# Two units' scores together in six PSUM banks: the order of scores and values in a top-k attention kernel with an MLP

## The chip, the cores and the metric

The kernel runs on one core of a Trainium2 chip. A core has a matrix engine (PE) that writes its results into PSUM, a vector engine (DVE), an activation engine (ACT), a general engine (POOL) and DMA queues, here all issued by the sync engine (SP). Each engine works through its own list of instructions in order and waits on semaphores for the others. PSUM has eight banks of 512 float32 per partition; a tile pool of the kernel hands them out in whole banks.

The metric is the device time of one execution in microseconds. The kernel before takes 1516.82 us (median of four runs, 1515.82 to 1518.07). The profile comes from one further look at the same program: that execution took 1517.07 us, of which 1515.2 us are the span that the profile shows.

## What is computed

Eight batches of eight heads, 576 queries and keys of 64 elements each. Of each row of scores the 32 largest are kept, the rest are masked; softmax, times the values; the heads side by side make a token of 512, and the 4608 tokens go through a leaky-ReLU MLP of width 2048. Everything is float32.

```python
scores = scale * np.matmul(q, k.transpose(0, 1, 3, 2))          # (8, 8, 576, 576)
kth = np.partition(scores, -32, axis=-1)[..., -32:-31]
scores = np.where(scores >= kth, scores, -1e9)
attn = np.exp(scores - np.max(scores, axis=-1, keepdims=True))
attn = attn / (np.sum(attn, axis=-1, keepdims=True) + 1e-09)
x = np.matmul(attn, v)                                          # to (4608, 512)
h = x @ w_in                                                    # 512 to 2048
out = np.maximum(0.01 * h, h) @ w_out                           # 2048 to 512
```

## The kernel before, in words

**Units.** The attention is cut into 144 units. A unit is a pair of heads and 128 queries (or 64 queries of two pairs, for the 64 queries that are left over in each batch). The steps of the main loop (`for s in range(...)`, L416) each work on several units at once: in step s, DVE selects the top 32 of unit s (`top_k`), POOL masks unit s-1 (`mask`), ACT takes exponents of unit s-1 (`exponents`, `sums`), normalises unit s-2 (`normalize`, after DVE's `reciprocals`) and splits it into 16-bit halves (`transpose`), which SP writes to DRAM and reads back transposed as `wT`. On every even step PE multiplies two transposed units with their values (`weigh_values`), ACT copies the result into the MLP's input (`keep_values`), and PE computes the scores of two later units, s+2 and s+3 (`scores`).

**Scores.** The two heads of a unit lie on rows 0 to 63 and 64 to 127 of the matrix engine and run side by side. Head i writes the tile `psc{i}`, two banks with 288 keys each, and ACT copies each head with one instruction of 576 columns into the unit's SBUF tile `s_sb`. There is one pair of these tiles (four banks), so the second unit's scores can't start before the first unit's copies are done. The kernel puts the values between the two: first unit's scores, values of two units, second unit's scores (L449 to L459).

**MLP.** `mlp` (L299) is a generator that issues a few matmuls at a time. For a chunk of 256 tokens (the first two have 128) it forms 16 hidden blocks: four matmuls into a bank `ph` (L307), then one ACT instruction `Prelu` into `gT` (L313). Then for each 128 tokens 16 matmuls of 512 columns into a bank `pz` (L319), an ACT copy to `o_sb` (L326) and a DMA out. A float32 matmul of the program stands in the trace as two MATMUL records. `mlp_steps` spreads these pieces over seven slots of each step, by a budget; five of the slots come before the scores and values of an even step, two after. PE therefore leaves a hidden block half done at a slot's end, does the scores and values, and takes it up again.

**Banks.** Four for the scores, one for the values (`ps_po`, tile `po`), three in turn for the MLP (`ps_ml`, tag `ml`). The MLP's next tile waits until ACT has emptied the tile three before it.

**Order.** The whole order is written by hand (`tc.manual_schedule`): each engine gets its instructions in the order of the program text. On ACT an even step reads: two normalisations (L250), the exponents of head 0 (L238), two splits (L259), the exponents of head 1 with the sums (L238, L243), then copies of scores and values, with the `Prelu` of each finished hidden block standing where its last matmuls were issued. So ACT can't empty a bank while it is still at an earlier normalisation or split.

**Before the loop** the MLP's weights, 16 pieces given as float64, are rounded to float32 (`round_weights`). The first 13 pieces use the score banks, the last three the MLP's. The scores of units 0 and 1 are issued at piece 14 of 0 to 15 (L409).

## Time and profile before

| What | Value |
|---|---|
| median of four runs | 1516.82 us |
| the profiled execution | 1517.07 us |
| its span | 1515.2 us |
| DVE busy | 1330.7 us (88%) |
| ACT busy | 1118.1 us (74%) |
| POOL busy | 1079.4 us (71%) |
| `ph` matmuls, L307 | 2432 records, 517.1 us |
| `pz` matmuls, L319 | 1152 records, 506.7 us |
| scores, L198 | 1280 records, 199.4 us; idle before them 28.3 us |
| values, L283 | 3200 records, 182.6 us; idle before them 20.4 us |
| `Prelu` of 256 columns, L313 | 272 of 380 ns |
| copy of 512 columns out of PSUM, L326 | 36 of 586 ns |
| copy of one head's scores, L207 | 288 of 639 ns |

Matmul records overlap: the engine takes the next one before the last has left its pipeline. The time that a matmul costs is therefore read from start to start, and a PE that shows as 100% busy may still hide gaps of a tenth of a microsecond.

### The profile page before, as it was taken

What the parts mean: (1) busy time and instruction counts of PE and PEld (TensorE: products, weight loads), DVE (VectorE), ACT (ScalarE), POOL (GpSimd) and SP (SyncE); (2) the same over time, 40 slices, a digit from 0 to 9 for tenths busy, and PEclk for the clock granted to TensorE, in tenths of its full rate; (3) what the DMA queues carried; (4) which work ended last, traced back from release to release, by engine and by line L of the source; (5) the groups of instructions that cost most, each with busy time, mean ns of one, the idle gap of its engine ahead of it and who ended that gap; (6) DMA issues with size and microseconds to landing.
All of it is one profiled execution on the core that took longest, in us unless ns stands there. A gap on an engine that the chain in (4) does not pass through costs nothing.

```text
span 1515.2 us, 24441 instructions
## 1 busy us (share of the span) xinstructions
PE 1431.4 (94%) x8192; PEld 952.6 (63%) x8192; DVE 1330.7 (88%) x3421; ACT 1118.1 (74%) x2141; POOL 1079.4 (71%) x726
## 2 busy tenths in 40 slices
PE   6736978999999999999999999999999999999998
PEld 2324665757676766575757676767676666666774
DVE  6799999999899998899999998999999989999600
ACT  7846787878787877687878787878787878787720
POOL 0068778887878777878787777777887878788700
PEclk9965989999999999999999999999999999999999
DMA  7714456555765455545655455645665456544510
GB/s 285 280 31 125 126 153 185 165 140 141 186 152 150 128 166 157 167 133 151 176 165 135 140 160 168 166 136 148 192 153 149 139 155 154 154 135 138 140 54 14
DMA packets 399294, 227.05 MB, mean 150 GB/s; under 512 B 343360, under 2 KB 343360, under 8 KB 397120
## 3 DMA queue, kind: packets, MB, share of 16 engines
q1 hardware_dynamic: 399168, 225.49, 53.3%
q8 instruction: 64, 1.05, 0.3%
q14 instruction: 62, 0.51, 0.1%
HBM read 46.14 MB, written 94.37 MB: 93 GB/s over the span
## 4 chain that ended last, share of the span: by engine, by line
PE 82%; DVE 11%; ACT 4%; DMA 2%; issue 1%; SPq 0%; POOL 0%; DVEq 0%; ACTq 0%; POOLq 0%
PE ph L307 31%; PE pz L319 30%; PE psc L198 10%; PE po L283 10%; DVE tops L221 4%; DVE pairs L224 3%; DVE pairs L216 1%; ACT split L259 1%; DMA raw<-in_weights_dram 1%; ACT s_sb L238 1%; ACT s_sb L250 1%; DVE scale L144 1%; ACT wT L121 0%; DVE w_out L147 0%; ACT scale L127 0%
## 5 line engine op out<-in xcount | busy, mean ns | idle before, releaser
L234 POOL TENSOR_SCALAR pen<-s_sb,tops 128x576 f32<-128x576 f32 x288 | 638.4, 2217 | 237.6 <-DVE tops L221 204.4
L221 DVE MAX8 tops<-pairs 128x8 f32<-128x288 f32 (+1 forms) x1152 | 635.5, 591 | 0.0
L307 PE MATMUL ph<-x,w_in 128*128 128x256 f32 (+1 forms) x2432 | 517.1, 372 | 6.4 <-ACT gT L313 6.4
L319 PE MATMUL pz<-w_out,gT 128*128 128x512 f32 x1152 | 506.7, 595 | 1.3 <-ACT gT L313 1.3
L307 PEld LDWEIGHTS ph<-x,w_in 128*128 128x128 f32 x2432 | 442.3, 192 | 87.0 <-issue 21.9
L224 DVE MATCH_REPLACE8 pairs<-tops,pairs 128x288 f32<-128x288 f32 (+1 forms) x864 | 459.8, 537 | 0.0
L235 POOL TENSOR_TENSOR s_sb<-s_sb,pen 128x576 f32<-128x576 f32 x288 | 406.8, 1413 | 24.0
L319 PEld LDWEIGHTS pz<-w_out,gT 128*128 128x128 f32 x1152 | 215.9, 190 | 265.4 <-issue 263.0
L259 ACT COPY split<-s_sb 128x1152 uint16<-128x1152 uint16 x288 | 315.6, 1144 | 0.0
L207 ACT COPY s_sb<-psc 128x576 f32<-128x576 f32 x288 | 169.3, 639 | 114.7 <-PE psc L198 114.7
L250 ACT ACTIVATE s_sb<-s_sb,rz 128x576 f32<-128x576 f32 x288 | 206.6, 767 | 31.8 <-DVE rz L247 31.7
L238 ACT ACTIVATE s_sb<-s_sb,nbias 128x576 f32<-128x576 f32 x288 | 221.1, 768 | 11.5 <-POOL s_sb L235 11.4
L198 PE MATMUL psc<-kt,qt 64*128 64x288 f32 (+1 forms) x1280 | 199.4, 442 | 28.3 <-ACT s_sb L207 27.8
L216 DVE TENSOR_TENSOR pairs<-s_sb 128x576 f32<-128x576 f32 x288 | 213.7, 780 | 10.2 <-DVE tops L221 0.5
L283 PE MATMUL po<-wT,vt 128*64 128x128 f32 (+1 forms) x3200 | 182.6, 271 | 20.4 <-DMA wT<-apart 19.6
L283 PEld LDWEIGHTS po<-wT,vt 128*64 128x64 f32 x3200 | 163.7, 141 | 52.2 <-issue 27.6
L313 ACT ACTIVATE gT<-ph 128x256 f32<-128x256 f32 (+1 forms) x304 | 107.3, 369 | 100.9 <-PE ph L307 100.6
L198 PEld LDWEIGHTS psc<-kt,qt 64*128 64x128 f32 (+1 forms) x1280 | 110.9, 182 | 100.4 <-ACT s_sb L207 37.2
L232 POOL TENSOR_SCALAR nbias<-tops 128x2 f32<-128x2 f32 x144 | 33.5, 233 | 92.3 <-DVE tops L221 79.5
L247 DVE RECIPROCAL rz<-ze 128x2 f32<-128x2 f32 x144 | 22.4, 155 | 74.4 <-ACT ze L243 73.8
L297 ACT COPY x<-po 128x128 f32<-128x128 f32 (+1 forms) x160 | 32.5, 264 | 65.6 <-PE po L283 65.6
L224 DVE MATCH_VALUE_LOAD pairs<-tops,pairs 128x8 f32 x864 | 62.0, 72 | 0.0
(38 smaller groups left out, 317.2 us busy)
## 6 DMA issues: line engine op xcount, KB each, us to landing
apart<-split SPq DMA_DIRECT2D x288, 288.0 KB, 2.1
raw<-in_weights_dram SPq DMA_DIRECT2D x16, 1024.0 KB, 5.0
vt<-in_vk_dram SPq DMA_DIRECT2D x32, 320.0 KB, 3.7
qt<-in_qT_dram SPq DMA_DIRECT2D x32, 288.0 KB, 3.6
kt<-in_kT_dram SPq DMA_DIRECT2D x32, 288.0 KB, 4.0
out_dram<-o_sb SPq DMA_DIRECT2D x36, 256.0 KB, 2.0
wT<-apart SPq DMA_TRANSPOSE x144, 4.6
```

Source lines behind the costliest of these rows:

```text
L198: nc.tensor.matmul(ps[i][r0:r0 + u.rows, half, 0:HS], qt[d, u.q0:u.q0 + u.rows], kt[d, half * HS:(half + 1) * HS], start=True, stop=True,)
L216: nc.vector.tensor_tensor(pairs[:, :, n, :], u.both[:, :, 0:HS], u.both[:, :, HS:S], op)
L221: nc.vector.max(out=u.tops[:, i, r, :], in_=rest[i])
L224: nc.vector.match_replace(out=rest[i], in_to_replace=u.tops[:, i, r, :], in_values=rest[i], imm_value=LOWEST)
L234: nc.gpsimd.tensor_scalar(pen, u.s[i], u.tops[:, i, ROUNDS - 1, 7:8], MASKED, ALU.is_lt, ALU.mult)
L235: nc.gpsimd.tensor_tensor(u.s[i], u.s[i], pen, ALU.add)
L238: nc.scalar.activation(u.s[i], u.s[i], AF.Exp, bias=u.nbias[:, i:i + 1], scale=SCALE, accum_out=u.z[:, i:i + 1])
L250: nc.scalar.activation(u.s[i], u.s[i], AF.Copy, bias=0.0, scale=u.rz[:, i:i + 1])
L259: nc.scalar.copy(split, pairs[:, :, h])
L283: nc.tensor.matmul(po[side * D:(side + 1) * D, o, :], vt[:, c, side, :], u.wT[:, c + side * NKC if c + 1 < NKC else c, r:r + n], start=(c ...
L307: nc.tensor.matmul(ph[:, 0:n], w_in[c][:, f * P:(f + 1) * P], x[c][:, 0:n], start=(c == 0), stop=(c == HP - 1),)
L319: nc.tensor.matmul(pz[0:m, 0:DMODEL], gT[f][:, r0:r0 + m], w_out[f // 4][:, f % 4, :], start=(f == 0), stop=(f == NFC - 1),)
```

## The change

The scores of an even step's two units are now issued together, after the values of that step. Each unit has a tile `wide` of two banks (one for each head, 352 keys; two buffers), and both share one tile `narrow` of two banks, in which each head's bank holds the remaining 224 keys of the first unit and of the second. ACT copies both heads of a unit with one instruction, first the two wide parts, then the two narrow ones.

The values have no bank of their own any more: `po` is taken from the MLP's pool, which has two buffers now. The MLP fills a bank with two hidden blocks (2 x 256 columns) and has one `Prelu` of 512 columns for both; `gT` is one tile. The generator still stops after every second matmul. The scores of units 0 and 1 are issued at piece 15.

```diff
-    ps_po = ctx.enter_context(tc.tile_pool(name="ps_po", bufs=1, space=bass.MemoryType.PSUM))
-    ps_ml = ctx.enter_context(tc.tile_pool(name="ps_ml", bufs=3, space=bass.MemoryType.PSUM))
+    ps_ml = ctx.enter_context(tc.tile_pool(name="ps_ml", bufs=2, space=bass.MemoryType.PSUM))
...
-    gT = [const.tile([P, CHMAX], F32, name=f"gT{f}") for f in range(NFC)]
+    gT = const.tile([P, NFC, CHMAX], F32, name="gT")
...
-            pw = ps_sc.tile([P, 2, 512], F32, name=f"psc{n % 2}")
+            pw = ps_sc.tile([P, 2, 512], F32, name="wide", bufs=2)
...
-    def scores(u):
-        ps = [ps_sc.tile([P, 2, 512], F32, name=f"psc{i}") for i in range(2)]
-        for n in range(0, len(u.parts), 2):
-            for half in range(2):
-                for i, pi, side, r0 in u.parts[n:n + 2]:
...
-        for i in range(2):
-            nc.scalar.copy(u.s[i].rearrange("p (h n) -> p h n", h=2), ps[i][:, :, 0:HS])
+    def scores(us):
+        narrow = ps_sc.tile([P, 2, 512], F32, name="narrow")
+        ps = {}
+        for k, u in enumerate(us):
+            wide = ps_sc.tile([P, 2, 512], F32, name="wide", bufs=2)
+            ps[u] = ((wide[:, :, 0:WIDE], 0, WIDE),
+                     (narrow[:, :, k * NARROW:(k + 1) * NARROW], WIDE, S))
+        for u in us:
+            for n in range(0, len(u.parts), 2):
+                for to, k0, k1 in ps[u]:
+                    for i, pi, side, r0 in u.parts[n:n + 2]:
...
+                        nc.tensor.matmul(to[r0:r0 + u.rows, i, :], qt[d, u.q0:u.q0 + u.rows],
+                                         kt[d, k0:k1], start=True, stop=True)
...
+        for part in range(2):
+            for u in us:
+                to, k0, k1 = ps[u][part]
+                nc.scalar.copy(u.both[:, :, k0:k1], to)
...
-        for f in range(NFC):
-            ph = ps_ml.tile([P, 512], F32, name="ph", tag="ml")
...
-            nc.scalar.activation(gT[f][:, 0:n], ph[:, 0:n], AF.Prelu, alpha=SLOPE)
+        for f0 in range(0, NFC, 2):
+            ph = ps_ml.tile([P, 2, CHMAX], F32, name="ph", tag="ml")
+            for i in range(2):
+                f = f0 + i
...
+                    if c == 1 or i == 0 and c == HP - 1:
+                        yield 2 * max(n, 225)
+            nc.scalar.activation(gT[:, f0:f0 + 2, 0:n], ph[:, :, 0:n], AF.Prelu, alpha=SLOPE)
...
-            elif n == NPIECE - 2:
-                for u in steps[0:2]:
-                    scores(u)
             elif n == NPIECE - 1:
+                scores(steps[0:2])
...
-            for u in new[:1]:
-                scores(u)
             if s % 2 == 0:
-                po = ps_po.tile([P, 2, P], F32, name="po")
+                po = ps_ml.tile([P, 2, P], F32, name="po", tag="ml")
...
                 attended(s)
-            for u in new[1:]:
-                scores(u)
+            if new:
+                scores(new)
```

## The prediction

> **What bounds the kernel now.** I read the page's busy times and its chain first, then the table of windows, then the timeline of PE in one stretch and of ACT beside PE in another.

> ```profile
> PE 1431.4 (94%) x8192; PEld 952.6 (63%) x8192; DVE 1330.7 (88%) x3421; ACT 1118.1 (74%) x2141; POOL 1079.4 (71%) x726
> PE 82%; DVE 11%; ACT 4%; DMA 2%; issue 1%; SPq 0%; POOL 0%; DVEq 0%; ACTq 0%; POOLq 0%
> ```
> ```profile
> 200.00:250.00 50.00, 40.71 (x302) 27.80 (x299) 49.27 (x132) 38.22 (x81) 42.85 (x29) 0.90 0.65 180
> 800.00:1000.00 200.00, 200.00 (x1230) 134.30 (x1229) 188.87 (x497) 156.77 (x310) 160.75 (x107) 1.00 0.54 152
> ```

> The columns of the second fence are PE, PEld, DVE, ACT and POOL busy, the granted clock, the DMA share and GB/s. Up to about 290 us DVE is nearly full and PE waits; from there PE is never idle, DVE idles 5%, and 98 matmuls of MLP are left for PE after the last unit. PE's list of work from 290 us on is the time. A change counts if it shortens or stretches that list.

> How dense is the list? Starts of PE's stretches in the timeline:

> ```profile
> 794.69 4.26 PE L307 MATMUL ph<-x,w_in 128*128 128x256 f32 x19
> 798.88 1.24 PE L198 MATMUL psc<-kt,qt 64*128 64x288 f32 x8
> ...
> 803.56 14.08 PE L307 MATMUL ph<-x,w_in 128*128 128x256 f32 x64
> 817.57 1.24 PE L198 MATMUL psc<-kt,qt 64*128 64x288 f32 x8
> 818.74 2.40 PE L283 MATMUL po<-wT,vt 128*64 128x128 f32 x40
> 821.07 1.24 PE L198 MATMUL psc<-kt,qt 64*128 64x288 f32 x8
> 822.25 2.86 PE L307 MATMUL ph<-x,w_in 128*128 128x256 f32 x12
> 824.94 5.31 PE L319 MATMUL pz<-w_out,gT 128*128 128x512 f32 x12
> ```

> (First and last row are cut by the window.) Let a be a `ph` matmul, e the extra time on entering another kind of tile, x that on leaving. 64a+e+x = 817.57-803.56 = 14.01; 19a+x = 798.88-794.69 = 4.19 (its entering lies outside); 12a+e = 824.94-822.25 = 2.69. So a = 0.216, e = 0.10, x = 0.09 us. A stretch of scores takes 1.17 us: four steps of two heads at 0.245 and 0.19 of entering and leaving.

> Next, ACT beside PE before another group of scores and values:

> ```profile
> 416.75 0.38 ACT L313 ACTIVATE gT<-ph 128x256 f32<-128x256 f32 x1 [0.55 <-PE ph L307]
> 417.03 1.43 ACT L250 ACTIVATE s_sb<-s_sb,rz 128x576 f32<-128x576 f32 x2
> 418.36 0.76 ACT L238 ACTIVATE s_sb<-s_sb,nbias 128x576 f32<-128x576 f32 x1
> ...
> 419.12 2.19 ACT L259 COPY split<-s_sb 128x1152 uint16<-128x1152 uint16 x2
> 420.09 1.24 PE L198 MATMUL psc<-kt,qt 64*128 64x288 f32 x8
> 421.21 0.66 ACT L313 ACTIVATE gT<-ph 128x256 f32<-128x256 f32 x2
> 421.26 2.40 PE L283 MATMUL po<-wT,vt 128*64 128x128 f32 x40
> ...
> 423.60 1.61 PE L198 MATMUL psc<-kt,qt 64*128 64x288 f32 x8
> ```

> The block of two normalisations, exponents and two splits holds ACT from 417.03 to 421.21, 4.18 us, in which no bank is emptied; two `Prelu` come out after it, though their matmuls ended long before. Three MLP banks just hide it. The last row shows the one price paid now: 1.61 in place of 1.24 us, since the second unit's scores waited 0.37 us for the first unit's copies.

> **The change, part by part** (62 groups of scores and values lie after 290 us).

> *One stretch of scores instead of two.* Before, a group goes MLP, scores, values, scores, MLP; after, MLP, values, scores, MLP. The eight steps stay; one entering and one leaving go: 0.19 us. 62 x 0.19 = -11.8 us. The nine or so groups before 290 us count nothing, PE waits there anyway (if they counted, -1.7 more).

> [...]

> *Widths 352 and 224 for 288 and 288.* At a per column (0.216/256) that is 0.297+0.189 against 2 x 0.243: nothing. If the narrow matmul kept the pace of 288, it costs 2 steps x 2 units x 0.056 = 0.22 us a group, +14 in all; at about 204 us 36 `ph` matmuls of 128 columns take 4.29 us, 0.12 each, so a short matmul does run faster than 0.19. I take 0.

> *The wait for the first unit's copies* goes: 11 of the 62 groups have the row of 1.61 us: 11 x 0.37 = -4.1 us. Nothing takes its place on PE, the score tiles were emptied a whole double step (18.9 us) before.

> *ACT.* The four copies move the same 2 x 1152 columns: 0. One `Prelu` of 512 columns costs as much as the copy of 512, 0.59 us (L326), against 2 x 0.38: 0.17 saved 152 times, 25 us of ACT. ACT isn't the bound: 0 on the path. Behind the group ACT now has four copies in a row in place of two; PE then finishes a half-done pair of hidden blocks first, which hides them; without that cover one group would pay up to 1.3 us.

> *Two banks for MLP and values.* Between pairs nothing changes: a bank was wanted again 2 blocks x 8a = 3.46 us after its last matmul, and still is, one pair later. New is that `po` takes an MLP bank. In the built program's order `po` waits, in 32 of 71 groups, for the `Prelu` of pair p that ended shortly before, and this `Prelu` stands on ACT directly behind the block of 4.18 us, which stands behind the `Prelu` of pair p-1. In 21 of them PE has half a pair (8 matmuls) to do in between, in 11 a quarter (4). In the other 39 the bank fell free 12 us before, or the group lies before 290 us. Worked out from S, the start of pair p's last matmul: pair p-1 ended 16a = 3.46 us before; a `Prelu` starts 0.42 us after its last matmul's start where ACT is free, so at S-3.04; the block starts 0.49 later (0.59 less an overlap of 0.10, as 416.75+0.38 and 417.03 show), S-2.55; it ends at S+1.63; `Prelu` p ends at S+2.22, PE sees it 0.05 later, S+2.27. PE would have been ready at S + 8a + a + x = S+2.04, or S + 4a + a + x = S+1.17. Waits: 0.23 x 21 + 1.10 x 11 = +16.9 us. Low end 0, if ACT gets to the block earlier than I see; high end: if `reciprocals` lets the block start late. DVE's waits for ACT's sums are 73.8 us in 48 times, 1.5 each, and in the row above the reciprocal ended 0.92 before the block; half a microsecond late in all 32 is +16 more.

> [...]

> *Values 1.2 us earlier*, as no scores stand before them. They wait for transposed weights and for v:

> ```profile
> 572.76 1.31 PE L283 MATMUL po<-wT,vt 128*64 128x128 f32 x20 [0.96 <-DMA wT<-apart]
> 632.89 0.80 PE L283 MATMUL po<-wT,vt 128*64 128x64 f32 x20 [0.83 <-DMA vt<-in_vk_dram]
> ```

> Both waits grow by what PE comes earlier: 2 x 1.2 = 2.4. With 4.6 us from a transpose's issue to its landing, nine more second units of a group had 0.4 to 1.2 us to spare; together they lack up to 2.5, and where `po` waits for a `Prelu` first, less: +0.8. Sum +3.2 (0 to 5).

> *Before the loop.* Pieces 13 to 15 share two banks instead of three, and the first scores' copies stand behind piece 15's ACT work instead of in front. DVE idled 2.6 us at 73 us behind those copies; that goes, and DVE then waits about as long for the last `scale` of piece 15, behind the copies. 0, within 2 either way.

> *Sum*: -11.8 - 4.1 + 16.9 + 3.2 = +4.2 us on the profiled 1517.07 (span 1515.2 to 1519.4): 1521.3. The runs' median is 0.25 lower: **1521 us**. A measurement tells 0.2%, 3 us, from no change.

> **Rivals.**
> - *The bank for the values is free in time* (faster). For it: ACT is 74% busy and loses 25 us of work. Against: 421.21 above, where ACT reaches the next `Prelu` 1.1 us after PE left the MLP. Without the +16.9: 1517.1-11.8-4.1+3.2 = 1504. It decides if `Prelu` p ends before S+1.17.
> - *The block itself starts late, behind the reciprocal* (slower): 16 more, 1537. For it: DVE waited 2.8 us for the sums just before 416 us. Against: 0.92 us of room there. It decides where the reciprocal ends later than S-2.55.
> - *Narrow matmuls no faster than 288 columns* (slower): 1521+14 = 1535. Against: the 0.12 us of 128 columns.

> That the change does not do what it says is out: the built order has the values first, then eight steps of both units, and the same matmuls of MLP between the groups.

> **How the numbers follow.** My case 0.52, the rivals 0.22, 0.20, 0.06. My case has terms of both signs, each good to a few us: 1513 to 1528, 0.30 slower by over 3 us, 0.21 within, 0.01 faster. The free bank is faster (0.21, 0.01 within), the other two slower. Faster 0.22, same 0.22, slower 0.56. The range cuts the outer half of the free bank's case and of the late block's: 1505 to 1534.

> **What would show it.** Right: values directly behind MLP, one row of 16 score matmuls of about 2.1 us; PE idle before `po` put down to ACT `gT`, some 30 times and 10 to 20 us; no wait of scores for copies after 290 us. Wrong: no such wait and a span near 1502; waits of over 1.5 us before `po`, with the normalisations released by DVE; a narrow matmul over 0.2 us from the next; or PE idle before `ph` for `gT`.

## The result, and the profile after

The changed kernel takes 1518.21 us (median of 31 runs, 1516.61 to 1520.74) against 1515.78 us for the kernel before (51 runs). The ratio is 1.0018, with a 95% interval from 1.0013 to 1.0023: some 2.4 us slower, inside what was called no change. (Slower by more than 3 us had been given 0.56, no change 0.22.) The profiled execution took 1518.61 us, with a span of 1516.8 us, so 1.5 us more than the profiled one before. The forecast of 1521 us held, with its range; why it was not 1518 is shown below.

First the same views as before: busy times and chain of the page, then two rows of the table of windows.

```profile
PE 1401.5 (92%) x8192; PEld 947.9 (62%) x8192; DVE 1332.1 (88%) x3421; ACT 1108.8 (73%) x1989; POOL 1079.3 (71%) x726
PE 72%; ACT 14%; DVE 7%; DMA 4%; issue 2%; SPq 0%; DVEq 0%; ACTq 0%
```
```profile
200.00:250.00 50.00, 40.91 (x305) 28.86 (x302) 45.94 (x124) 36.08 (x69) 39.54 (x27) 0.87 0.58 155
800.00:1000.00 200.00, 196.39 (x1202) 133.25 (x1199) 186.65 (x488) 153.92 (x284) 158.59 (x106) 1.00 0.54 148
```

PE was full between 800 and 1000 us, now it idles 3.6 us of 200, and the chain runs through ACT for 14% instead of 4%. PE's busy time fell by 30 us, and the span didn't. What it waits for stands in the table of waits of PE from 290 us on (line, releaser, us in total, times, longest):

```profile
PE po L291 <- ACT gT L323: 15.0, 31, 1.0
PE po L291 <- DMA wT<-apart: 1.9, 3, 0.9
```

31 waits of the values for a `Prelu`: the forecast had 32, of 16.9 us. PE's timeline has one of the longer ones, and ACT's timeline what stands in front of it:

```profile
493.73 3.19 PE L317 MATMUL ph<-x,w_in 128*128 128x256 f32 x14
497.95 2.40 PE L291 MATMUL po<-wT,vt 128*64 128x128 f32 x40 [1.04 <-ACT gT L323]
500.29 0.86 PE L207 MATMUL wide<-kt,qt 64*128 64x352 f32 x4
500.98 0.54 PE L207 MATMUL narrow<-kt,qt 64*128 64x224 f32 x4
501.36 0.76 PE L207 MATMUL wide<-kt,qt 64*128 64x352 f32 x4
501.95 0.54 PE L207 MATMUL narrow<-kt,qt 64*128 64x224 f32 x4
502.43 1.78 PE L317 MATMUL ph<-x,w_in 128*128 128x256 f32 x7
```
```profile
492.63 0.60 ACT L323 ACTIVATE gT<-ph 128x512 f32<-128x512 f32 x1 [0.65 <-PE ph L317]
493.13 1.43 ACT L258 ACTIVATE s_sb<-s_sb,rz 128x576 f32<-128x576 f32 x2
494.46 0.77 ACT L246 ACTIVATE s_sb<-s_sb,nbias 128x576 f32<-128x576 f32 x1
...
495.21 2.19 ACT L267 COPY split<-s_sb 128x1152 uint16<-128x1152 uint16 x2
497.31 0.59 ACT L323 ACTIVATE gT<-ph 128x512 f32<-128x512 f32 x1
```

The `Prelu` of 497.31 is ready to run when PE has done its pair, but ACT is in its block from 493.13 to 497.31, 4.18 us. PE has nothing left that it may do before the values, and starts them 0.05 us after the `Prelu` ends. The scores then run in one row of 16 matmuls in 502.43-500.29 = 2.14 us; the two narrow steps of the first unit take 0.38 us (500.98 to 501.36), the two wide ones of the second 0.59.

For all groups, the time from the start of the last MLP matmul before a group to the start of the first one after it, read out of the traces, medians for groups of two units of 128 queries; the sum goes over the 62 groups that the forecast counted:

| | groups amid `ph` | groups amid `pz` | sum of 62 |
|---|---|---|---|
| before | 4.99, in 11 of them 5.35 | 5.20 | 318.8 us |
| after | 5.03, in 9 of them 5.90 | 5.00 | 318.1 us |

Amid `pz` no `Prelu` is late, and the one stretch shows its gain, 0.20 us. Amid `ph` the wait has eaten it. All groups together became 0.7 us shorter, and the `ph` matmuls between them 1.2 us. The 1.5 us come from the time before: the first of the 62 groups starts 3.4 us later. Here is the first instruction of that group, in the kernel before and in the changed one:

```profile
308.21 1.24 PE L198 MATMUL psc<-kt,qt 64*128 64x288 f32 x8
```
```profile
311.64 2.40 PE L291 MATMUL po<-wT,vt 128*64 128x128 f32 x40
```

1.9 of the 3.4 us are there when DVE begins its first `pairs`, at 80.49 us, before at 78.58. The rest is added between 80 and 290 us.

### The profile page after: what moved, and what is told of

It reads as the page before. It is cut to its first block, busy times and chain, and to the rows that moved or that the text cites. A ratio compares the mean times of both kernels' runs of the same rounds, so it can differ in the third digit from the quotient of the medians.

```text
span 1516.8 us, 24415 instructions
## 1 busy us (share of the span) xinstructions
PE 1401.5 (92%) x8192; PEld 947.9 (62%) x8192; DVE 1332.1 (88%) x3421; ACT 1108.8 (73%) x1989; POOL 1079.3 (71%) x726
## 3 DMA queue, kind: packets, MB, share of 16 engines
q8 instruction: 64, 1.05, 0.3%
## 4 chain that ended last, share of the span: by engine, by line
PE 72%; ACT 14%; DVE 7%; DMA 4%; issue 2%; SPq 0%; DVEq 0%; ACTq 0%
PE pz L329 30%; PE ph L317 21%; PE po L291 11%; PE wide L207 6%; ACT split L267 6%; ACT s_sb L258 4%; PE narrow L207 3%; DMA wT<-apart 2%; DVE tops L229 2%; ACT s_sb L246 2%; DVE pairs L232 2%; DMA apart<-split 1%; ACT gT L323 1%; DMA raw<-in_weights_dram 1%; DVE pairs L224 1%
## 5 line engine op out<-in xcount | busy, mean ns | idle before, releaser
L317 PE MATMUL ph<-x,w_in 128*128 128x256 f32 (+1 forms) x2432 | 511.7, 370 | 5.3 <-ACT gT L323 5.3
L215 ACT COPY s_sb<-wide 128x704 f32<-128x704 f32 x144 | 107.4, 746 | 50.7 <-PE wide L207 45.6
L323 ACT ACTIVATE gT<-ph 128x512 f32<-128x512 f32 (+1 forms) x152 | 86.6, 571 | 76.7 <-PE ph L317 76.7
L207 PE MATMUL wide<-kt,qt 64*128 64x352 f32 (+1 forms) x640 | 120.7, 493 | 0.0
L207 PE MATMUL narrow<-kt,qt 64*128 64x224 f32 (+1 forms) x640 | 80.8, 354 | 0.7 <-ACT s_sb L215 0.7
L207 PEld LDWEIGHTS narrow<-kt,qt 64*128 64x128 f32 (+1 forms) x640 | 56.6, 180 | 32.3 <-issue 1.8
```

The costliest lines, as they stand in the source:

```text
L207: nc.tensor.matmul(to[r0:r0 + u.rows, i, :], qt[d, u.q0:u.q0 + u.rows], kt[d, k0:k1], start=True, stop=True)
L317: nc.tensor.matmul(ph[:, i, 0:n], w_in[c][:, f * P:(f + 1) * P], x[c][:, 0:n], start=(c == 0), stop=(c == HP - 1),)
```

## The experiments

Ratios are to the kernel before, run beside each on the same chip; a group's time is that defined above.

**e1: the values' sums out of the MLP's banks.** The wide tiles have columns 352 to 512 free; the sums go into 128 of them, in the second unit's tile.

```diff
+    def wide_tiles():
+        return [ps_sc.tile([P, 2, 512], F32, name="wide", bufs=2) for k in range(2)]
...
-    def scores(us):
+    def scores(us, wides=None):
+        wides = wides or wide_tiles()
...
-                po = ps_ml.tile([P, 2, P], F32, name="po", tag="ml")
+                wides = wide_tiles()
+                po = wides[1][:, :, WIDE:WIDE + P]
...
-                scores(new)
+                scores(new, wides)
```

> The values' sums move out of the MLP's two banks into the unused columns 352 to 480 of the second new unit's wide score tile; everything else as in the changed kernel. Theory (the values wait for a Prelu behind ACT's block, 22.6 us in 35 waits): these waits go, up to 3 us come back as waits for transposed weights, so 1518 - 22.6 + 0 to 3, about 1497 (1494 to 1502). Rival (the wait is only moved, to the transposed weights or to the second unit's scores, which now stand behind the copies of the values in the same tile): 1513 to 1518.

Measured: 1499.44 us (1494.13 to 1503.88, 6 runs), ratio 0.9895 (0.9877 to 0.9913). Groups amid `ph` take 4.78 us, amid `pz` 5.00, the sum is 301.3, 16.8 us less than in the changed kernel. PE's waits from 290 us on:

```profile
PE wide L293 <- DMA wT<-apart: 2.0, 2, 1.2
```

```profile
493.86 14.08 PE L319 MATMUL ph<-x,w_in 128*128 128x256 f32 x64
507.87 2.40 PE L293 MATMUL wide<-wT,vt 128*64 128x128 f32 x39
```

The waits for a `Prelu` are gone and did not move; the values now follow 64 `ph` matmuls after 14.01 us, what the forecast had as the time of 64 without a wait. (The window ends within the values.) This kernel beats both, and lies in the theory's range. Its profile is 6 us ahead of the changed kernel's already at 290 us, where the forecast had counted the groups as free; its executions scatter by 10 us, so how much of that is steady stays open.

**e2: the same banks, but the MLP stops only between pairs.**

```diff
-                    if c == 1 or i == 0 and c == HP - 1:
-                        yield 2 * max(n, 225)
...
-            yield 2 * max(n, 225)
+            yield 8 * max(n, 225)
```

(The second line is the one behind the `Prelu`.)

> The MLP gives way only after a whole pair of hidden blocks, so that no half-done pair holds a bank at a group and the values take the bank that fell free one pair earlier. Theory: the 22.6 us of waits for Prelu go as well, 1497 to 1502, with the values still in the MLP's two banks. Rival (it is two banks for MLP and values as such, with the pair or without): 1513 to 1520, with the wait now in front of the next pair.

Measured: 1508.15 us, ratio 0.9955 (0.9944 to 0.9967), sum of groups 310.5 us. The waits for a `Prelu` are gone, as the theory says, but both ranges were missed. The groups gained 7.6 us where e1 gained 16.8; the rest went into a wait that neither named here (e1's rival had): for transposed weights, 6.7 us in nine times, and for v, 1.0 in two. PE's waits for the weights, then PE and ACT around the longest:

```profile
PE po L291 <- DMA wT<-apart: 6.7, 9, 1.9
```
```profile
798.53 14.08 PE L317 MATMUL ph<-x,w_in 128*128 128x256 f32 x64
812.54 1.31 PE L291 MATMUL po<-wT,vt 128*64 128x128 f32 x20
815.77 1.31 PE L291 MATMUL po<-wT,vt 128*64 128x128 f32 x20 [1.91 <-DMA wT<-apart]
```
```profile
802.29 0.60 ACT L321 ACTIVATE gT<-ph 128x512 f32<-128x512 f32 x1 [2.40 <-PE ph L317]
802.79 1.43 ACT L258 ACTIVATE s_sb<-s_sb,rz 128x576 f32<-128x576 f32 x2
```

The block of the odd step, which makes the second unit's transposed weights, stands on ACT behind the `Prelu` of the first pair after a group. That pair now begins only after the group (798.53), so ACT idles 2.40 us for it and the block is late. From the end of the last split to the values of that unit there are 6.61 us at the least in this kernel, under 6.81 in a quarter of the groups; in the changed kernel 8.27 at the least.

**e3: the changed kernel's banks with PE's order of before.** `scores` calls the values between its two units.

```diff
-        for u in us:
+        for j, u in enumerate(us):
+            if j:
+                between()
             for n in range(0, len(u.parts), 2):
```

> The changed kernel's banks and copies, but PE's order of before in a group: scores of one unit, values, scores of the other. Theory: the values come 1.17 us later, which covers the waits of 0.22 and 1.12 us for Prelu (-22.6), and one more entering and leaving costs 62 x 0.19 = +11.8: about 1507 (1504 to 1512), faster than the changed kernel. Rival (one stretch is all gain, and the wait for the Prelu would be there in any order): 1518 + 11.8 = 1530.

Measured: 1509.05 us, ratio 0.9961 (0.9948 to 0.9974), within the theory's range. Groups take 4.99 and 5.20 us, the sum is 313.8. In these banks, one stretch in place of two makes the kernel slower: it brings the values 1.17 us forward, into ACT's block.

**e4: the first scores back at the last piece but one.**

```diff
-            elif n == NPIECE - 1:
+            elif n == NPIECE - 2:
                 scores(steps[0:2])
```

> The changed kernel with the first two units' scores put back to the last piece but one of the weights, as before. Theory (the start lost 1.9 us because DVE waited 3.7 us for the last scale behind the first scores' copies): -1.9, 1516.3. Rival (the start has slack, PE's list from 290 us on decides): 1518, no change.

Measured: 1516.18 us (11 runs), ratio 1.0006 (0.9997 to 1.0014) against 1.0018 (1.0013 to 1.0023). DVE's timeline, the changed kernel and then this one:

```profile
78.49 0.69 DVE L145 TENSOR_TENSOR scale<-scale,top 128x1024 uint16<-128x1024 uint16 x1 [3.68 <-ACT scale L128]
79.29 1.29 DVE L148 TENSOR_TENSOR w_out<-pw,scale 128x512 f32<-128x512 f32 x2
80.49 1.42 DVE L224 TENSOR_TENSOR pairs<-s_sb 128x576 f32<-128x576 f32 x2
```
```profile
77.35 0.69 DVE L148 TENSOR_TENSOR w_out<-pw,scale 128x512 f32<-128x512 f32 x1 [0.60 <-PE pw L143]
77.96 1.42 DVE L224 TENSOR_TENSOR pairs<-s_sb 128x576 f32<-128x576 f32 x2
```

The wait of 3.68 us goes, DVE starts 2.5 us earlier, and the time is about 1.8 us lower (1.0018-1.0006, of 1516). The two intervals just overlap: the gain is shown for DVE's start and likely for the time.

**e5 and e9: the price of the second stretch alone.** e5 is e1 with the order of e3.

> The values' sums in the wide tile, as in e1_po_in_wide, with PE's order of before: scores of one unit, values, scores of the other. No wait for a Prelu is there in either, so this is the price of the second entering and leaving alone. Theory: 62 x 0.19 = +11.8 on e1_po_in_wide, 1511 (1508 to 1514), by the groups' own durations 0.2 us each. Rival (the gain of one stretch came from elsewhere): 1499 to 1503.

Measured: 1544.78 us, ratio 1.0195 (1.0180 to 1.0210); both were wrong. PE's waits, and a group on its timeline:

```profile
PE wide L211 <- ACT x L309: 32.9, 60, 0.7
```
```profile
501.55 2.40 PE L295 MATMUL wide<-wT,vt 128*64 128x128 f32 x40
504.49 0.86 PE L211 MATMUL wide<-kt,qt 64*128 64x352 f32 x4 [0.53 <-ACT x L309]
```

The second unit's scores now follow directly on the values, in the same tile, and wait until ACT has copied the sums out: 0.55 us on the mean, 60 times. In e1 the first unit's scores lie between and hide it. e9 takes the first unit's tile.

```diff
-                po = wides[1][:, :, WIDE:WIDE + P]
+                po = wides[0][:, :, WIDE:WIDE + P]
```

> e5_wide_split with the values' sums in the first unit's wide tile in place of the second's, so that the second unit's scores no longer stand behind the copies of the values. Theory (e5_wide_split was 45 us over e1_po_in_wide by 33 us of that wait and 12 us of the second entering and leaving): the 33 go, 62 x 0.19 stay, 1499 + 12 = 1511 (1508 to 1514). Rival (splitting the stretch costs more than the entering and leaving, whatever it waits for): 1520 or more.

Measured: 1505.01 us, ratio 0.9924 (0.9910 to 0.9937). The wait is gone (1.0 us once for weights, 0.9 for keys remain). Groups take 4.99 and 5.20 against 4.78 and 5.00 us in e1, the sum 313.9 against 301.3: +12.6, of which 11.5 are the same 0.1 to 0.2 us in each of 59 groups and 1.1 longer waits for transfers in two. The times differ by less, 0.9924-0.9895 = 0.0029 or 4.4 us with an uncertainty of some 3, and 1505 lies below the range given. Where the rest went is open; the spans of the two profiles differ by 10.5 us (1504.5 and 1494.0), e1's being one of the shorter of its executions.

**e6: e1 and e4 together.** 

> e1_po_in_wide with the first scores at the last piece but one of the weights. Theory (the start and the groups add up): e4_scores_earlier took 1 to 2.5 us off the changed kernel, so 1497.5 (1496.5 to 1498.5). Rival (once the waits in the groups are gone, DVE decides between 80 and 290 us and the start is hidden): 1499.5.

Measured: 1495.31 us (1494.22 to 1496.12), ratio 0.9867 (0.9852 to 0.9881), the fastest kernel here, 23 us below the changed one. That is below the range given (1496.5 to 1498.5); by the ratios the two gains add up within the uncertainty.

**e7: single blocks in two banks**, otherwise e1.

```diff
-        for f0 in range(0, NFC, 2):
-            ph = ps_ml.tile([P, 2, CHMAX], F32, name="ph", tag="ml")
+        for f in range(NFC):
+            ph = ps_ml.tile([P, 512], F32, name="ph", tag="ml")
...
-            nc.scalar.activation(gT[:, f0:f0 + 2, 0:n], ph[:, :, 0:n], AF.Prelu, alpha=SLOPE)
+            nc.scalar.activation(gT[:, f, 0:n], ph[:, 0:n], AF.Prelu, alpha=SLOPE)
```

> e1_po_in_wide with one hidden block of 256 columns a bank and a Prelu for each, in two banks, instead of pairs. Theory (the pair is what lets two banks hide ACT's block of 4.2 us; with single blocks a bank is wanted again one block, 0.87 us, after its last matmul): some 2.7 us for each of ACT's blocks beside hidden blocks, about 54 of them, +100 to +200 on 1499. Rival (two banks are enough with or without pairs): 1499 to 1505, the 25 us of ACT being off the path.

Measured: 1546.5 us (2 runs), ratio 1.0205 (1.0184 to 1.0226), +47 us on e1. Right in kind, half the size at most. PE's waits, and ACT beside a block:

```profile
PE ph L317 <- ACT gT L323: 30.6, 28, 1.7
```
```profile
504.63 1.43 ACT L260 ACTIVATE s_sb<-s_sb,rz 128x576 f32<-128x576 f32 x2
506.08 0.38 ACT L323 ACTIVATE gT<-ph 128x256 f32<-128x256 f32 x1
506.36 0.77 ACT L248 ACTIVATE s_sb<-s_sb,nbias 128x576 f32<-128x576 f32 x1
```

With a `Prelu` for each block, one falls between normalisations and exponents and cuts ACT's block in two. The waits are 28 of 1.1 us on the mean, not 54 of 2.7. They are 31 of the 51 us between the two profiles; 12 are there at 290 us already, and 8 were not followed up.

**e8: the kernel before, values in the MLP's pool of four banks.**

```diff
-    ps_po = ctx.enter_context(tc.tile_pool(name="ps_po", bufs=1, space=bass.MemoryType.PSUM))
-    ps_ml = ctx.enter_context(tc.tile_pool(name="ps_ml", bufs=3, space=bass.MemoryType.PSUM))
+    ps_ml = ctx.enter_context(tc.tile_pool(name="ps_ml", bufs=4, space=bass.MemoryType.PSUM))
```

(`po` then comes from `ps_ml` with the tag `ml`.)

> The kernel before with the values' sums taken from the MLP's pool, which then has four banks of single blocks. Theory (sharing costs only where the rotation hands the values a bank whose Prelu stands behind ACT's block; with four banks it is the bank of four blocks ago, 3 x 0.87 us after its last matmul, and 1.17 us of scores stand before the values too): half of ACT's block is covered, 0 to +8 on 1515. Rival (sharing as such costs 0.3 us a group or more, whatever the number of banks): +17 or more.

Measured: 1511.78 us (11 runs), ratio 0.9977 (0.9968 to 0.9986): 3.5 us faster, below the theory's 0. Groups take what they took before (4.99, 11 of 5.35, 5.20), with no wait for a `Prelu`. The profile is 3.3 us ahead by 290 us and 6.0 at the end; the early part fits a fourth bank for the last pieces of the weights, which was not tried alone. With four banks, and scores in front of the values, sharing cost these groups nothing.

**e10 and e11: ACT's block made longer**, in the changed kernel and in e1.

```diff
                 transpose(older)
+                if s % 2 == 0:
+                    for k in range(2):
+                        nc.scalar.copy(spare, w_in[k][:, 0:352])
```

> The changed kernel with two more copies on ACT (352 columns of w_in each, into a spare tile that nobody reads) behind the splits of every even step: ACT's block in front of the Prelu gets about 0.7 us longer, nothing else depends on them. Theory (the values stand directly behind that Prelu in 31 to 35 groups): 0.7 x 33 = +23, 1541 (1535 to 1546). Rival (ACT, 73% busy, has room for 50 us more, and the waits come from elsewhere): 1518 to 1522.

> The same two copies in e1_po_in_wide, where the values don't wait for a Prelu. Theory: 0 to +3 on 1499 (1496 to 1503), the same 50 us of ACT being hidden there. Rival (ACT's load as such slows the list): +20.

Measured: e10 1555.02 us, ratio 1.0259 (1.0241 to 1.0276), +36.8 us on the changed kernel and 9 above the theory's range; e11 1497.94 us, ratio 0.9880 (0.9867 to 0.9894), e1's time within the uncertainty. ACT and PE in e10, then PE's waits:

```profile
506.69 1.00 ACT L453 CAST spare<-w_in 128x352 bf16<-128x352 f32 x2
507.60 0.59 ACT L324 ACTIVATE gT<-ph 128x512 f32<-128x512 f32 x1
```
```profile
508.24 2.40 PE L292 MATMUL po<-wT,vt 128*64 128x128 f32 x40 [1.95 <-ACT gT L324]
```
```profile
PE po L292 <- ACT gT L324: 43.1, 31, 2.0
```

The copies take 0.91 us (506.69 to 507.60), not 0.7. The same 31 waits grow by (43.1-15.0)/31 = 0.91 us each: the block reaches PE one to one. That is 28 of the 37 us; most of the rest is in the last section. In e11 the same work of ACT costs nothing that shows (1497.94 us against e1's 1499.44).

## Why the forecast held, and what in it did not

*What bounds the kernel.* Right: PE's list from 290 us on. Lengthening ACT alone is free in e11 (1497.94 us against 1499.44), and the 16.8 us that e1 takes off PE's groups are there in the runs (18.8). The 12.6 us between e9 and e1 are there only in part, 4.4.

*One stretch, -11.8.* Right in size: 0.20 us a group, -11.5 over the 59 of the 62 groups that have scores, from the groups of e9 and e1 that wait for nothing. So one entering and one leaving cost 0.20 us in these groups.

*Widths, 0.* Right: 0.38 and 0.59 us for two steps are 0.97, against 4 x 0.245 = 0.98 before.

*The wait for the first unit's copies, -4.1.* Right, and a little small: the 11 groups of 5.35 us are gone, and 1.5 us more in three groups of other shapes, -5.6 in all. e5 shows the same kind of wait come back when copies and scores share a tile without work between them (32.9 us in 60 times).

*ACT 25 us lighter, 0 on the path.* The `Prelu` fell by 20.7 us (107.3 to 86.6), the copies of scores rose by 8.3 (169.3 to 177.6), and ACT's busy time fell by 9.3 in all. It didn't matter, as e11 says.

*Two banks, +16.9.* Right in place and size: 15.0 us in 31 waits, +17.1 by the lengths of the groups over those of e1, waits of 1.04 us and groups of 5.03 us (0.25 over e1's 4.78) where 1.10 and 0.23 were worked out. e10 shows it is ACT's block, e3 that 1.17 us of other work in front hides it. e1 cures it with no bank more (0.9895), and e8, with four banks, shares without harm (0.9977): what counts here is whether the bank handed out was emptied before ACT's block.

That between the pairs nothing changes was 1.2 us off: before, 22 steps from one `ph` matmul to the next, away from the groups, took 0.23 to 0.34 us instead of 0.216, and after none. What held them was not followed up.

*Values 1.2 us earlier, +3.2.* Wrong in place and sign. Groups lengthened by late transfers had cost 3.8 us before (2.7 in one by weights and keys, 1.05 in another by v); after, 3.1, all by weights, in four other groups (0.6, 0.3, 1.1, 1.0): -0.7. The forecast moved every group's margin by 1.2 us. But stopping points and ACT's block moved as well: between the last split and the second unit's values the shortest time rose from 7.3 to 8.27 us while the median fell from 9.38 to 8.59. Why just these four groups are late now, no run shows. e2 shows the term when the margin falls everywhere.

*Before the loop, 0.* Mis-sized: +1.9 at DVE's first `pairs`. DVE's wait for the last `scale` was seen, but taken as equal to the one that goes; it is 3.68 against 2.60 us, and 0.74 for PE comes with two banks. The groups before 290 us, which the forecast counted as nothing, made +3.4 of it. e4 takes 1.8 back.

Together from 290 us on: -11.5-5.6+17.1-0.7-1.2 = -1.9; with +3.4 before, the sum is +1.5, what the profiles have. So the forecast's +4.2 was too high by 3.9 for the late transfers, by 1.5 for the copies and by 1.2 between the pairs, and too low by 3.4 at the start; the other terms were good to 0.3. That 1521 lies within 3 us of the result is in part luck: these errors have both signs.

Of the rivals, the bank that is free in time gave 1504; e1 made it true and gives 1499. The late block (1537) is out: the longest wait is 1.04 us. Slow narrow matmuls (1535) are out by the rows of the scores.

## What to carry to other kernels

Ask of a shared buffer not how many there are but which instruction empties the one handed out next, and what stands in front of that on its in-order engine (here 4.18 us of ACT's block in front of a `Prelu`); then move the tile, not the work (e1, 18.8 us less). Unused columns of a bank that is busy anyway can hold a small sum, if other work lies between its copy and the next use of the tile (it does in e1; in e5 it does not, and PE waited 0.55 us 60 times). An engine that is a quarter idle on the mean can still be the wait in half of the groups (ACT in the changed kernel: 73% busy, 31 waits in 62 groups).

## What the runs showed of the hardware

```profile
814.89:818.30 3.41, 1.46 (x22) 1.11 (x22) 3.41 (x10) 3.17 (x7) 3.23 (x3) 1.00 0.78 274
818.30:821.71 3.41, 3.41 (x28) 2.83 (x26) 3.41 (x12) 0.43 (x2) 3.26 (x2) 0.50 0.57 117
835.37:838.78 3.41, 2.00 (x10) 1.42 (x8) 3.38 (x7) 3.38 (x7) 2.43 (x2) 1.00 0.84 224
838.78:842.19 3.41, 2.87 (x44) 2.60 (x46) 3.41 (x14) 1.86 (x6) 3.31 (x2) 1.00 0.41 118
```

In each of the five the wait lies inside one cell of the grid, PE is busy there for 1.46 or 1.47 us, and the clock is 0.50 for the next cell. In each of the six an edge of the grid cuts the wait, the emptier cell still has 1.7 to 2.0 us of work, and the clock stays at 1.00. Between 290 and 1480 us the traces of the kernel before and of the changed one have no cell with less than 2.37 us of work, and no drop. Before 290 us the border is not sharp: in the kernel before, a cell with 1.47 us (from 206.53 us) was followed by no drop, one with 1.66 (from 192.87) by one. So in e10 whether a wait of 1.95 us brought the clock down hung on how it lay to the grid.

By the lengths of their values and scores the drops cost 8.3 us in these five groups. In the profiles the 62 groups of e10 take 34.4 us more than the changed kernel's: 27 from the waits, 8.3 from the drops, and 1.0 less from late transfers. A further 5.8 us are there before the first of them. (This execution is the longest of e10's four, so the profiles differ by 40 us and the medians by 37.) The changed kernel's eleven waits of 1.04 us left the values at 2.33 to 2.42 us.
